# Retention in 64x64 tiles four at a time, and the layout of heads that goes with it

## The chip, the cores and the metric

The kernel runs on one core of a Trainium2 chip. A core has TensorE (PE, whose weight loads the profile lists apart as PEld), VectorE (DVE), ScalarE (ACT), GpSimd (POOL) and SyncE (SP), which issues the transfers between device memory and the on-chip memory SBUF. Matrix products land in PSUM, eight banks of 512 fp32 values in each of 128 partitions. The metric is the device time of one execution in microseconds; the time before is 725.04 us, the median of 4 runs (723.75 to 725.8).

## What is computed

Two blocks follow one another. First retention, with 4 batches, 8 heads, 768 positions and head size 64; then a gated feed-forward block over 3072 tokens of width 512 with 1536 hidden features.

```python
for t in range(S):
    state = gamma * state + einsum('bhd,bhe->bhde', k[:, :, t], v[:, :, t])
    y[:, :, t] = scale * einsum('bhd,bhde->bhe', q[:, :, t], state)
x = y.transpose(0, 2, 1, 3).reshape(B * S, H * D)
g = x @ w_gate
out = (g * sigmoid(g) * (x @ w_val)) @ w_out
```

q, k and v are fp32. The weights are float64 and reach the kernel as pairs of 32-bit words.

## The kernel before

**Retention by chunks.** The 768 positions of a batch are six chunks of 128. For a chunk, `scores` (L379) computes k times q per head into two banks (L385) and VectorE multiplies them by a table of decays (L391). `mix` (L431) computes y: the old state times q (L442, for all chunks but a batch's first), then the chunk's own v times scores (L446), which accumulates onto it; ScalarE copies y to the tile `xT` (L449), the input of the second block. `state` (L414) updates the running state (L424, L427, L429). Heads come in pairs: head 2n + i is at partitions 64i to 64i + 63 of pair n. A matmul of L385 has 64 rows and 128 columns of weights, one of L442 64 and 64, one of L446 and L424 128 and 64. Each fp32 matmul leaves two records in the profile, with two weight loads.

**Segments and stages.** The 24 chunks form four segments of six, three positions each of two batches. The program starts with retention of segment 0. Then the first up stage, `up(f)` for 12 blocks of hidden features, computes the products with w_gate and w_val (L515) by a scheme that needs seven products of sums of blocks where plain multiplication needs eight. A `down` stage multiplies by w_out by the same scheme (L709, L718). Later up stages, `up2`, apply the scheme twice (L626). Retention of segment s + 1 runs within the down stage of segment s: after each product `down` calls `step()`, and at counts listed in `DUE` (L841) `step()` runs one piece of `retention` (L453): scores of chunk n + 1, then mix, decay and state of chunk n. `sums_x` (L487) forms the sums of blocks of x on VectorE; in segment 0 it reads y from PSUM.

**Weights.** A piece of w_gate and w_val (128 hidden features, 1 MB in float64) is loaded by `load_piece` (L192), on SP's queue. It is turned to fp32 in three parts: `convert_a` on ScalarE (absolute value L242, copies of the sign words to two banks L246, low words L249), `convert_b` on VectorE (L259, L261, L265), `convert_c` on GpSimd (L274). Then `sums_t` on VectorE (L289) forms the sums of weight blocks, and `keep_wt` (L149) stores them to device memory for the later stages. The pieces of w_out take the same way.

**Order.** It is written out by hand: the string at L835 for segment 0 (s, m, t, x for scores, mix, state, sums; a, b, c, B, S, C, T for the parts of the conversion; the number is the chunk or the piece) and the table `beside` (L320) for the first up stage, whose entries run between products. Every engine works through its own instructions in that order, so an instruction that waits holds up those behind it. SP issues loads in order too, and a load into a buffer waits for GpSimd to be done with the buffer's last piece.

**Banks.** `bank(tag)` (L99) hands out banks in turn: scores 4 and 5, state 6, y 7, and 2 and 3 for the products wb and z of the down stage (L726, L758). In segment 0, y of the six chunks is in banks 0, 1, 2, 3, 7 and 6 (L436).

Of the kernel before, what the change touches and what calls it, by code (L numbers as in the profile page):

```python
# [12 lines left out]
U32 = mybir.dt.uint32  # L13
# [28 lines left out]
def tile_retnet_swiglu(  # L42
# [56 lines left out]
    def bank(tag):  # L99

        own = {"x": (0, 1), "wz": (2, 3), "s": (4, 5), "st": (6,), "y": (7,)}[tag]
        turn[tag] = turn.get(tag, -1) + 1
        return banks[own[turn[tag] % len(own)]]
# [88 lines left out]
    def load_piece(piece):  # L192

        kind, a, h = piece
        if kind == "up":
            new_wt(a)
            gate, val = (w[:, ts(a, P)].rearrange("(c p) f -> p c f", p=P)
                         for w in (w_gate, w_val))
            parts = [(val[:, ds(KH, KH)], 0), (val[:, ds(0, KH)], 1), (gate, 2)]
        else:  # L200
            top, low = (w_out[ts(a + FH * i, P)] for i in range(2))
            parts = ([(low[:, DH:], 0), (top[:, DH:], 1)],
                     [(top[:, :DH], 0), (low[:, :DH], 1)])[h]
        to, slot, n = span(piece)
        to = to[:, ds(slot, n)]
        if w_gate.dtype != F32:
# [4 lines left out]
        for src, i in parts:  # L211
            if w_gate.dtype != F32:
                src = src.bitcast(U32)
            if len(src.shape) == 3:
                c = src.shape[1]
                t = to[:, i:].rearrange("p a b -> p (a b)")[:, : c * src.shape[2]]
                t = t.rearrange("p (c f) -> p c f", c=c)
            else:
                t = to[:, i]
            nc.sync.dma_start(out=t, in_=src)  # L220
# [15 lines left out]

    def convert_a(piece, own, part=None):

        if piece in raw:
            d, lo, hi = words_of(piece)  # L240
            if part in (0, None):
                nc.scalar.activation(d, hi.bitcast(F32), AF.Abs)  # L242
            if part in (1, None):
                signs[piece] = []
                for i, o in enumerate(own):
                    nc.scalar.copy(banks[o], hi[:, ts(i, 512)].bitcast(F32))  # L246
                    signs[piece].append(banks[o])
            if part in (2, None):
                nc.scalar.activation(lo.bitcast(F32), lo, AF.Copy, scale=2.0 ** -51,  # L249
                                     bias=2.0)  # L250
# [18 lines left out]
    def convert_c(piece, halves=1):  # L269
        if piece in raw:  # L270
            d, lo, hi = words_of(piece)
# [107 lines left out]
    def scores(c):  # L379
        kt, qt = (pairs(t) for t in chunks[c][:2])  # L380
        sp = [bank("s") for i in range(2)]
        for n in range(NP):
            for i in range(2):
                r = ds(D * i, D)
                nc.tensor.matmul(sp[i][:, ts(n, P)], kt[r, n], qt[r, n],  # L385
                                 start=True, stop=True, skip_group_check=True)
# [27 lines left out]
    def state(c):  # L414
# [5 lines left out]
        st = bank("st")[:, : NP * D].rearrange("p (n e) -> p n e", n=NP)  # L420
# [552 lines left out]
```

## Time and profile before

| what | value |
|---|---|
| median of 4 runs | 725.04 us (723.75 to 725.8) |
| the profiled execution's own time | 724.39 us |
| its span | 722.6 us |
| TensorE: busy, share, instruction records | 708.0 us, 98%, 4544 |
| VectorE | 466.9 us, 65% |
| ScalarE | 240.0 us, 33% |
| GpSimd | 239.4 us, 33% |
| moved by DMA | 139.06 MB, mean 192 GB/s |

The span runs from the first to the last instruction of the program. The page says how long each engine was busy, and the chain of waits says what work, followed back from the end, set the time. A line such as L385 names the line of the kernel that issued an instruction. In a row of the timeline the bracket tells how long the engine was idle before, and what it then waited for. The granted clock of TensorE is full throughout.

In time order: segment 0's retention to 30 us, the first up stage to 149 us, the down stages (with retention) at 149 to 223, 319 to 395, 491 to 568 and 664 to 719 us, and the later up stages between them.

### The profile page before, as it was taken

The numbers are of one execution on the slowest core, as the hardware profiler recorded it, in microseconds if no ns is written. First come the engines' busy times: TensorE is split into PE (matmuls) and PEld (weight loads), VectorE is DVE, ScalarE is ACT, GpSimd is POOL, SyncE is SP. The second block draws the span as 40 slices with busy tenths as digits, with TensorE's granted clock in tenths as the row PEclk, the third lists the DMA queues.
The fourth block names the chain that finished last, engine by engine and source line by source line (L and its number), as shares of the span: only waits on it lengthen the run. The fifth ranks groups of instructions, "written<-read, shape, count | busy, mean of one in ns | idle before, by whom it ended". The sixth has DMA issues, their size and how long they took to land.

```text
span 722.6 us, 11724 instructions
## 1 busy us (share of the span) xinstructions
PE 708.0 (98%) x4544; PEld 616.5 (85%) x4544; DVE 466.9 (65%) x836; ACT 240.0 (33%) x484; POOL 239.4 (33%) x147
## 2 busy tenths in 40 slices
PE   7898999999999999999999999999999999999997
PEld 7654555578889999998888999998888999999886
DVE  3887998686858887875354575656652656667420
ACT  2668777411212232421121333331121233243000
POOL 0334444513101727470220445372210072735000
PEclk9999999999999999999999999999999999999999
DMA  9797897805997967742722555550473155630010
GB/s 320 241 376 266 281 295 223 312 14 189 393 351 278 332 208 268 240 168 88 257 94 102 182 202 206 198 182 16 139 255 132 59 200 200 203 134 1 9 51 30
DMA packets 60825, 139.06 MB, mean 192 GB/s; under 512 B 4577, under 2 KB 27617, under 8 KB 60769
## 3 DMA queue, kind: packets, MB, share of 16 engines
q1 hardware_dynamic: 57312, 132.01, 53.2%
q10 hardware_dynamic: 3456, 6.29, 2.3%
q8 instruction: 36, 0.59, 0.3%
q14 instruction: 21, 0.16, 0.1%
HBM read 101.72 MB, written 36.57 MB: 191 GB/s over the span
## 4 chain that ended last, share of the span: by engine, by line
PE 93%; DVE 1%; ACT 1%; issue 0%; DVEq 0%
PE bank L626 40%; PE bank L709 26%; PE bank L515 14%; PE bank L718 4%; PE bank L385 3%; PE bank L446 3%; PE bank L442 2%; PE bank L424 1%; DVE ring L289 0%; DVE iop L591 0%; ACT bank L246 0%; DVE hT L665 0%; ACT loadp L249 0%; DVE ring L265 0%; DVE ring L261 0%
## 5 line engine op out<-in xcount | busy, mean ns | idle before, releaser
L626 PE MATMUL bank<-loadp,ring 128*128 128x192 f32 x720 | 140.3, 327 | 0.0
L709 PE MATMUL bank<-wot,hsp 128*128 128x256 f32 x576 | 129.8, 382 | 0.0
L709 PEld LDWEIGHTS bank<-wot,hsp 128*128 128x128 f32 x576 | 108.0, 190 | 15.8 <-issue 0.5
L626 PEld LDWEIGHTS bank<-loadp,ring 128*128 128x128 f32 x720 | 120.6, 190 | 1.0 <-ACT midp L591 0.7
L591 DVE TENSOR_TENSOR iop<-bank,iop 128x384 f32<-128x384 f32 x144 | 79.6, 555 | 56.4 <-PE bank L626 53.0
L626 PE MATMUL bank<-xs,ring 128*128 128x192 f32 x432 | 87.9, 326 | 0.0
L661 POOL TENSOR_TENSOR hT<-iop 128x768 f32<-128x768 f32 x36 | 67.1, 1863 | 34.8 <-DVE iop L591 34.8
L591 ACT COPY hsp<-bank 128x384 f32<-128x384 f32 x90 | 43.0, 479 | 100.3 <-PE bank L626 89.5
L626 PEld LDWEIGHTS bank<-xs,ring 128*128 128x128 f32 x432 | 73.2, 190 | 0.0
L591 POOL TENSOR_TENSOR iop<-hsp,midp 128x768 f32<-128x768 f32 x9 | 16.3, 1814 | 165.7 <-ACT hsp L591 137.2
L626 PE MATMUL bank<-xT,ring 128*128 128x192 f32 x324 | 66.2, 327 | 0.8 <-DVE iop L591 0.8
L515 PE MATMUL bank<-xs,ring 128*128 128x384 f32 x192 | 64.7, 488 | 2.2 <-DVE xs L498 1.7
L709 PE MATMUL bank<-wot,hT 128*128 128x256 f32 x288 | 65.5, 381 | 0.0
L515 PEld LDWEIGHTS bank<-xs,ring 128*128 128x128 f32 x192 | 36.1, 190 | 28.9 <-issue 2.3
L709 PEld LDWEIGHTS bank<-wot,hT 128*128 128x128 f32 x288 | 54.3, 190 | 7.6 <-issue 0.2
L626 PE MATMUL bank<-hsp,ring 128*128 128x192 f32 x288 | 56.7, 326 | 0.5 <-ACT hsp L591 0.5
L626 PEld LDWEIGHTS bank<-xT,ring 128*128 128x128 f32 x324 | 54.8, 190 | 2.0 <-DVE iop L591 1.8
L515 PE MATMUL bank<-xT,ring 128*128 128x384 f32 x144 | 49.4, 488 | 1.5 <-DVE hT L552 1.5
L626 PEld LDWEIGHTS bank<-hsp,ring 128*128 128x128 f32 x288 | 48.4, 190 | 0.8 <-ACT hsp L591 0.8
L591 DVE TENSOR_TENSOR midp<-bank,midp 128x384 f32<-128x384 f32 x72 | 39.8, 554 | 13.8 <-PE bank L626 12.4
L768 DVE TENSOR_TENSOR iop<-bank,iop 128x256 f32<-128x256 f32 x12 | 5.1, 424 | 65.2 <-PE bank L709 48.2
L449 ACT COPY xT<-bank 128x512 f32<-128x512 f32 x24 | 14.1, 586 | 97.6 <-PE bank L446 97.6
(146 smaller groups left out, 987.0 us busy)
## 6 DMA issues: line engine op xcount, KB each, us to landing
ring<-unitt SPq DMA_DIRECT2D x50, 896.0 KB, 4.7
unitt<-ring SPq DMA_DIRECT2D x21, 896.0 KB, 6.0
unitb<-ring SPq DMA_DIRECT2D x12, 896.0 KB, 7.3
ring<-unitb SPq DMA_DIRECT2D x21, 512.0 KB, 6.0
out_dram<-iop ACTq DMA_DIRECT2D x24, 256.0 KB, 2.4
loadp<-in_w_val_dram SPq DMA_DIRECT2D x18, 256.0 KB, 3.7
loadp<-in_w_gate_dram SPq DMA_DIRECT2D x9, 512.0 KB, 6.5
midp<-in_w_out_dram SPq DMA_DIRECT2D x12, 256.0 KB, 6.6
```

The lines of the kernel that those rows point to most:

```text
L385: nc.tensor.matmul(sp[i][:, ts(n, P)], kt[r, n], qt[r, n], start=True, stop=True, skip_group_check=True)
L424: nc.tensor.matmul(st[ds(D * i, D), n], kd[:, h], vn[:, h], start=(n == 0), stop=True, skip_group_check=True)
L442: nc.tensor.matmul(y[r, ts(n, P)], prev[r, n], qd[r, n], start=(n == 0), stop=False, skip_group_check=True)
L446: nc.tensor.matmul(y[ds(D * i, D), ts(n, P)], vn[:, ts(2 * n + i, D)], a[i][:, n], start=(ci == 0 and n == 0), stop=True, skip_group_check ...
L449: nc.scalar.copy(xT[:, :, c // NCK % 2, ts(ci % L, P)], pairs(y))
L515: nc.tensor.matmul(o, w[:, slot, k], a[:, k], start=(start and k == 0), stop=(stop and k == KH - 1), skip_group_check=True)
L591: events.append((t, len(events), lambda: fn(*args, **kw)))
L626: nc.tensor.matmul(o[:, h], w[:, h, slot], rhs, start=(start and h == 0), stop=True, skip_group_check=True)
L661: by_block(9.5, 13.5, lambda r: pool(to[:, r], u2[:, r], p5[:, r], op=add))
L709: nc.tensor.matmul(o, a[:, k], wot[k][:, slot], start=(start and k == 0), stop=(k == FH - 1), skip_group_check=True)
L718: nc.tensor.matmul(o, a_dn(0, 0, u)[:, k], wot[k][:, B11], start=(k == 0), stop=(k == FH - 1), skip_group_check=True)
L768: tt(ev[0][:, DH:], wb, u2, op=ALU.add)
```

## The change

`scores` and the old state's part of `mix` issue matmuls of 64 rows and 64 columns of weights, so that four of them, two halves of the rows by two halves of the columns, follow one another. Scores are 16 instructions per chunk instead of 8; the others keep their number. y is in two banks, one for each i, of 256 columns each. In it, head 2n + i with n = 2h + b stands at partitions 64h, block b of bank i. `xT` takes this order, with one copy per bank. So the rows of w_gate and w_val are loaded in the same order: four transfers of 64 partitions for a piece instead of three of 128. `convert_a` works by halves of 512 columns that put the blocks of a half in their place, and writes the low words' result into the place of the high words. Banks are handed out anew: y has 6 and 7, state 6 for the first four chunks and 3 after that, wb and z of the down stage both 2; in segment 0 two chunks share a pair of banks.

```diff
@@ -98,7 +98,8 @@
 
     def bank(tag):
 
-        own = {"x": (0, 1), "wz": (2, 3), "s": (4, 5), "st": (6,), "y": (7,)}[tag]
+
+        own = {"s": (4, 5), "y": (6, 7)}[tag]
         turn[tag] = turn.get(tag, -1) + 1
         return banks[own[turn[tag] % len(own)]]
 
@@ -194,30 +195,34 @@
         kind, a, h = piece
         if kind == "up":
             new_wt(a)
-            gate, val = (w[:, ts(a, P)].rearrange("(c p) f -> p c f", p=P)
-                         for w in (w_gate, w_val))
-            parts = [(val[:, ds(KH, KH)], 0), (val[:, ds(0, KH)], 1), (gate, 2)]
-        else:
-            top, low = (w_out[ts(a + FH * i, P)] for i in range(2))
-            parts = ([(low[:, DH:], 0), (top[:, DH:], 1)],
-                     [(top[:, :DH], 0), (low[:, :DH], 1)])[h]
         to, slot, n = span(piece)
         to = to[:, ds(slot, n)]
-        if w_gate.dtype != F32:
+        bits = w_gate.dtype != F32
+        if bits:
             t = raw_places[kind].pop(0)
             if kind == "down" or a:
                 raw_places[kind].append(t)
             to = raw[piece] = t.bitcast(U32).rearrange("p (a b) -> p a b", a=n)
-        for src, i in parts:
-            if w_gate.dtype != F32:
-                src = src.bitcast(U32)
-            if len(src.shape) == 3:
-                c = src.shape[1]
-                t = to[:, i:].rearrange("p a b -> p (a b)")[:, : c * src.shape[2]]
-                t = t.rearrange("p (c f) -> p c f", c=c)
-            else:
-                t = to[:, i]
-            nc.sync.dma_start(out=t, in_=src)
+        parts = []
+        if kind == "up":
+
+
+            for w, i in ((w_val, 0), (w_gate, 2)):
+                w = w[:, ts(a, P)].rearrange("(h b j d) f -> h d b j f", h=2, b=2, j=2)
+                for h in range(2):
+                    t = to[ds(D * h, D), ds(i, 2)].rearrange("p i (b f) -> p i b f", b=2)
+                    if bits:
+                        parts.append((t.rearrange("p i b f -> p (i b) f"),
+                                      w[h].rearrange("d b j f -> d (b j) f")))
+                    else:
+                        parts += [(t[:, 1 - j if i == 0 else j], w[h][:, :, j])
+                                  for j in range(2)]
+        else:
+            top, low = (w_out[ts(a + FH * i, P)] for i in range(2))
+            parts = ([(to[:, 0], low[:, DH:]), (to[:, 1], top[:, DH:])],
+                     [(to[:, 0], top[:, :DH]), (to[:, 1], low[:, :DH])])[h]
+        for t, src in parts:
+            nc.sync.dma_start(out=t, in_=src.bitcast(U32) if bits else src)
 
 
 
@@ -234,20 +239,45 @@
         r = raw[piece].rearrange("p a (n two) -> p (a n) two", two=2)
         return d, r[:, :, 0], r[:, :, 1]
 
+    def by_half(piece):
+
+        d, lo, hi = words_of(piece)
+        for i in range(d.shape[1] // 512):
+            to, *src = (a[:, ts(i, 512)] for a in (d, lo, hi))
+            if piece[0] == "up":
+                to = to.rearrange("p (j b f) -> p j b f", j=2, b=2)
+                src = [a.rearrange("p (b j f) -> p j b f", j=2, b=2) for a in src]
+                if i == 0:
+                    src = [backwards(a) for a in src]
+            yield to, *src
+
+    def backwards(a):
+        (part, rows), (step, n), *rest = a.ap
+        return bass.AP(a.tensor, a.offset + step * (n - 1), [[part, rows], [-step, n], *rest])
+
     def convert_a(piece, own, part=None):
 
         if piece in raw:
             d, lo, hi = words_of(piece)
             if part in (0, None):
-                nc.scalar.activation(d, hi.bitcast(F32), AF.Abs)
+                for to, _, src in by_half(piece):
+                    nc.scalar.activation(to, src.bitcast(F32), AF.Abs)
             if part in (1, None):
                 signs[piece] = []
-                for i, o in enumerate(own):
-                    nc.scalar.copy(banks[o], hi[:, ts(i, 512)].bitcast(F32))
+                for o, (to, _, src) in zip(own, by_half(piece)):
+                    t = banks[o]
+                    if piece[0] == "up":
+                        t = t.rearrange("p (j b f) -> p j b f", j=2, b=2)
+                    nc.scalar.copy(t, src.bitcast(F32))
                     signs[piece].append(banks[o])
             if part in (2, None):
-                nc.scalar.activation(lo.bitcast(F32), lo, AF.Copy, scale=2.0 ** -51,
-                                     bias=2.0)
+
+                for i, (_, src, _) in enumerate(by_half(piece)):
+                    t = hi[:, ts(i, 512)]
+                    if piece[0] == "up":
+                        t = t.rearrange("p (j b f) -> p j b f", j=2, b=2)
+                    nc.scalar.activation(t.bitcast(F32), src, AF.Copy, scale=2.0 ** -51,
+                                         bias=2.0)
 
     def convert_b(piece, part=None):
 
@@ -268,7 +298,7 @@
 
     def convert_c(piece, halves=1):
         if piece in raw:
-            d, lo, hi = words_of(piece)
+            d, _, lo = words_of(piece)
             n = d.shape[1] // halves
             for i in reversed(range(halves)):
                 nc.gpsimd.tensor_tensor(d[:, ts(i, n)].bitcast(I32),
@@ -380,10 +410,11 @@
         kt, qt = (pairs(t) for t in chunks[c][:2])
         sp = [bank("s") for i in range(2)]
         for n in range(NP):
-            for i in range(2):
-                r = ds(D * i, D)
-                nc.tensor.matmul(sp[i][:, ts(n, P)], kt[r, n], qt[r, n],
-                                 start=True, stop=True, skip_group_check=True)
+            for h in range(2):
+                for i in range(2):
+                    r, m = ds(D * i, D), ds(D * h, D)
+                    nc.tensor.matmul(sp[i][m, ts(n, P)], kt[r, n, m], qt[r, n],
+                                     start=(n == 0), stop=True, skip_group_check=True)
         a = []
         for i in range(2):
             j = turn["a"] = turn.get("a", -1) + 1
@@ -417,7 +448,8 @@
             return
         vn, kd = chunks[c][2:]
         new = state_of(c)
-        st = bank("st")[:, : NP * D].rearrange("p (n e) -> p n e", n=NP)
+        st = banks[6 if c in first_chunks[:4] else 3][:, : NP * D]
+        st = st.rearrange("p (n e) -> p n e", n=NP)
         for n in range(NP):
             for i in range(2):
                 h = ts(2 * n + i, D)
@@ -432,23 +464,35 @@
         ci = c % NCK
         qd, vn = pairs(chunks[c][1]), chunks[c][2]
         a = att.pop(c)
-
-        y = banks[(0, 1, 2, 3, 7, 6)[first_chunks.index(c)]] if c in first_chunks else bank("y")
+        if c in first_chunks:
+
+            k = first_chunks.index(c)
+            y = [banks[b][:, ds(256 * (k % 2), 256)]
+                 for b in ((0, 1), (2, 3), (6, 7))[k // 2]]
+        else:
+            y = [bank("y")[:, :256] for i in range(2)]
+
+
+        y = [t.rearrange("p (b t) -> p b t", b=2) for t in y]
         if ci:
             prev = state_of(c, 1)
-            for n in range(NP):
-                for i in range(2):
-                    r = ds(D * i, D)
-                    nc.tensor.matmul(y[r, ts(n, P)], prev[r, n], qd[r, n],
-                                     start=(n == 0), stop=False, skip_group_check=True)
-        for n in range(NP):
+            for b in range(2):
+                for h in range(2):
+                    for i in range(2):
+                        r, n = ds(D * i, D), 2 * h + b
+                        nc.tensor.matmul(y[i][ds(D * h, D), b], prev[r, n], qd[r, n],
+                                         start=(b == 0), stop=False, skip_group_check=True)
+        for b in range(2):
             for i in range(2):
-                nc.tensor.matmul(y[ds(D * i, D), ts(n, P)], vn[:, ts(2 * n + i, D)],
-                                 a[i][:, n], start=(ci == 0 and n == 0), stop=True,
-                                 skip_group_check=True)
-        nc.scalar.copy(xT[:, :, c // NCK % 2, ts(ci % L, P)], pairs(y))
+                for h in range(2):
+                    n = 2 * h + b
+                    nc.tensor.matmul(y[i][ds(D * h, D), b], vn[:, ts(2 * n + i, D)],
+                                     a[i][:, n], start=(ci == 0 and b == 0), stop=True,
+                                     skip_group_check=True)
+        for i in range(2):
+            nc.scalar.copy(xT[:, ds(KH * i, KH), c // NCK % 2, ts(ci % L, P)], y[i])
         if c in first_chunks:
-            att[c] = pairs(y)
+            att[c] = y
 
     def retention(s):
 
@@ -491,7 +535,7 @@
 
         def b(i, h):
             y = att.get(first_chunks[2 * j + i])
-            return a(i, h) if y is None else y[:, ds(KH * h, KH)]
+            return a(i, h) if y is None else y[h]
 
         s1, s2, s3, s4 = (t[:, :, ts(j, P)] for t in xs)
         tt = nc.vector.tensor_tensor
@@ -723,7 +767,7 @@
                 step()
 
         def second(u):
-            z = bank("wz")[:, :DH]
+            z = banks[2][:, :DH]
             product(z, B21, a_dn(0, 1, u))
             to = iop[:, ts(2 * (u % 2), DM)]
             tt(to[:, :DH], z, first_dn.pop(u), op=ALU.add)
@@ -755,7 +799,7 @@
         elif u == 2 and s:
             first(u)
         cur = dict(hs)
-        wb = bank("wz")[:, :DH]
+        wb = banks[2][:, :DH]
         product(wb, T1, cur[1])
         p5 = tmp(2)
         nc.scalar.copy(p5, wb)
```

## The prediction

> **What bounds the kernel now.** I read the page's rows of the 40 slices first, then the chain of waits, then the work by ten-microsecond stretches, then ScalarE's timeline where weights arrive.
>
> ```profile
> span 722.6 us, 11724 instructions
> PE 708.0 (98%) x4544; PEld 616.5 (85%) x4544; DVE 466.9 (65%) x836; ACT 240.0 (33%) x484; POOL 239.4 (33%) x147
> PEclk9999999999999999999999999999999999999999
> ```
>
> TensorE is busy for 98% of the span at the full granted clock. Busy is not yet bound, so the chain of waits follows, for two steps of retention in the first down stage:
>
> ```profile
> 165.87 1.09 PE bank L385 x16
> 166.96 1.02 PE bank L442 x16
> 167.98 1.02 PE bank L446 x16
> 169.00 0.46 PE bank L424 x16
> 169.47 5.38 PE bank L709 x24
> ```
>
> Every piece is TensorE's own: scores (L385), old state's part of y (L442), the chunk's own part (L446), state (L424), then the down product. Whatever is saved here moves the end. The start and the first products are different. By stretches (us, then PE, PEld, DVE, ACT, POOL busy, clock, DMA share, GB/s):
>
> ```profile
> 30.00:40.00 10.00, 8.28 (x25) 4.67 (x26) 6.85 (x14) 5.93 (x10) 3.46 (x2) 1.00 0.76 234
> 40.00:50.00 10.00, 10.00 (x31) 5.35 (x30) 9.76 (x15) 6.64 (x11) 2.73 (x1) 1.00 1.08 374
> 50.00:60.00 10.00, 9.75 (x31) 5.43 (x29) 7.82 (x15) 6.46 (x10) 2.41 (x1) 1.00 0.95 324
> 60.00:70.00 10.00, 8.22 (x24) 4.39 (x24) 8.13 (x17) 9.26 (x15) 3.81 (x2) 1.00 0.83 280
> 70.00:80.00 10.00, 10.00 (x32) 6.00 (x32) 9.86 (x19) 8.03 (x15) 4.99 (x4) 1.00 0.82 270
> ```
>
> DMA is full (share 1.08) from 36 to 56 us, and PE idles 1.7 us in 30 to 40 and 1.8 us in 60 to 70. Who waits for DMA there, on ScalarE:
>
> ```profile
> 22.64 1.17 ACT L242 ACTIVATE ring<-loadp 128x1024 f32<-128x1024 f32 x1 [2.33 <-DMA loadp<-in_w_gate_dram]
> 28.69 1.18 ACT L242 ACTIVATE ring<-loadp 128x1024 f32<-128x1024 f32 x1
> 38.01 1.16 ACT L242 ACTIVATE ring<-loadp 128x1024 f32<-128x1024 f32 x1 [1.50 <-DMA loadp<-in_w_gate_dram]
> 43.42 1.16 ACT L242 ACTIVATE ring<-hsp 128x1024 f32<-128x1024 f32 x1
> ```
>
> These are the conversions of weight pieces 0 to 3. Pieces 0 and 2 wait for their load, and by the landing times in the trace (22.53, 28.47, 37.90, 43.31 us) pieces 1 and 3 are used within 0.25 us of landing. Pieces 4 and 5 land at 49.87 and 56.13 and are used at 53.77 and 57.35; from piece 6 on, a load has 4.4 to 7.7 us to spare. So a later load of the first four pieces is a later ScalarE, and behind its conversion in the same queue stand the copies that release TensorE (L449, L536, L541).
>
> **The change, part by part.**
>
> *Scores and old state.* The start times of single records tell how tiles overlap. Each fp32 matmul leaves two records. In L442 two 64x64 tiles start 7 ns apart and the next two 109 ns later; L446 (128x64) gives 109 ns as well, L385 (64x128) 111.6. Entering another tile shape costs more: 160 ns from the first pair to the second with 64 weight columns, 214 with 128, and 206 from the last pair to the next group. This rebuilds the rows: L385 is 214 + 6 x 111.6 + 206 = 1.09 us, L442 160 + 6 x 109 + 206 = 1.02.
> After, scores are 16 instructions per chunk, and both groups go in sets of four tiles. Two row tiles at once are shown by L385, two column tiles at once by L446; four at once are shown by no row. Lower bound: the set takes 109 ns. Upper: two pairs, 218. I take 112, since the second tile costs 7 ns of start only. Scores are then no faster in their eight sets, but their shape is now that of L442, and the change of shape between them goes: 160 + 6 x 109 + 109 = 0.92. L442 halves: 3 x 109 + 206 = 0.53. Together 1.46 instead of 2.11: 0.65 less. Scores alone save 0.07 (160 + 6 x 109 + 206 = 1.02), L442 alone 0.44 (160 + 2 x 109 + 206 = 0.58).
> Segments 1 and 3 have one step with scores alone, five with both, one with L442 alone: 0.07 + 5 x 0.65 + 0.44 = 3.8 us each. Segment 2, whose first two chunks have no old state, saves 3 x 0.07 + 3 x 0.65 + 0.44 = 2.6. Sum 10.2; at 112 ns for its 208 sets 0.6 less, 9.6. In the first down stage DMA share is 0.9 to 1.0 from 180 to 220 us and the last unit sum (VectorE L170) starts at 217.63 on a load landed at 214.61, so some of its 3.8 us is given back: I take 9.0. The first segment's six chunks count nothing: they wait for loads (TensorE's waits of 1.3 and 1.0 us for q_t).
>
> *Heads of y in two banks.* 24 copies of 128x512 (586 ns) become 48 of 128x256 (370 ns, as L761): 0.15 us per chunk on ScalarE, idle at L449 for 97.6 us in all: nothing. In the first segment two chunks now share two banks, so the second's y waits for the first's copies. For chunk 1 that is some 0.7 us before a wait of 1.3 us for q_t; for chunk 5 about 1 us, but its copy stands behind piece 1's conversion on ScalarE (28.69 to 30.88). Uncovered it would be 1 us; I take nothing.
> The down stage's wb and z now share bank 2 instead of alternating. z must follow VectorE's read of wb (L768), and the next wb the read of z (L729). The tightest places: L768 ends at 677.92, z starts at 679.81; L729 ends at 683.03, the next product starts at 684.99; in segment 0, 152.68 against 153.95. The cover is the product in between (2.7 us); without it 0.4 us each. Nothing.
>
> *Conversion by halves.* Two ScalarE operations of 512 for one of 1024, twice per piece: 2 x 0.56 against 1.06 from start to start, 0.1 us per piece, felt only where ScalarE sets the pace (60.2 to 64.5 us): 0.3 in all. VectorE and GpSimd do the same work.
>
> *Weight rows in another order.* A piece of 1 MB was 2 transfers of 256 KB and 1 of 512 KB over 128 partitions; it is now 4 of 256 KB, each to 64 partitions. SP issues one more (0.47 us) per piece, with room: it waits 35.6 us for GpSimd. What matters is the rate. By the row: in the full queue one 256 KB transfer lands 0.67 to 0.75 us after the one before (374 GB/s in 40:50); at that rate a piece stays at 2.8 us and costs nothing. The Trainium skill, "SBUF — State Buffer", section "Door 1: The DMA port swizzle", speaks against it: partitions 0 to 63 reach only 8 of 16 ports, measured 196 GB/s, at most 218; the section "Can I just issue two DMAs to hit both halves?" adds that a transfer to each half side by side brought +6%. No transfer of this trace goes to 64 partitions. By the rule 256 KB takes 262144 / 218 = 1.20 us (1.34 at 196), a piece 4.8, 2.0 more (2.5). I take the rule at 218.
> Transfers of the full queue land in the order of their issue, so each piece moves the later ones by 2.0:
> - Piece 0 lands at 24.5, piece 1 at 32.4 (was 28.47). From there ScalarE needs 0.6 (second half of the first conversion), 1.1 (signs) and 0.7 (chunk 5's copies), VectorE 0.45 (L498): the first T1 product starts at 35.3 where it started at 33.18, 2.1 late.
> - Piece 2 is issued after piece 0's last conversion, so 1.9 late, and lands at 37.9 + 1.9 + 2.0 = 41.8; 40.1 is wanted, and ScalarE's gaps there (0.8, and 0.6 ahead of TensorE) take most. Piece 3 lands behind it and a unit store (2.7): 41.8 + 2.7 + 4.8 = 49.3, wanted at 43.4 + 2.1 = 45.5; 3.8 late, 0.8 of it taken by the gap: +3.0.
> - Piece 4 lands 6.6 + 2.0 after piece 3, at 57.9, wanted at 53.8 + 5.1 = 58.9: in time. Piece 5 lands 6.3 + 2.0 after it, at 66.2, wanted at 57.4 + 5.1 = 62.5: 3.7 late, less 1.7 us of ScalarE idle before L246 and the 0.8 of PE's own wait: +1.2. From piece 6 on within slack.
> Sum 6.3, and all products behind follow one another on TensorE, so nothing takes it back. Ends: 0 and 11 (196 GB/s, no slack).
>
> *Sum.* -9.0 + 0.3 + 6.3 = -2.4. The profiled execution took 724.39 (span 722.6 and 1.8 around it), 0.65 under the median 725.04. Against the median: 722.6.
>
> **The rivals.**
> - *The half-partition transfers keep the rate of the row.* For: the old rate of 374 GB/s is itself not the ports' full rate, and neighbours in the queue may fill the other half. 725.04 - 9.0 + 0.3 = 716.3.
> - *Slower: the weight loads cost more than the packing saves.* One mechanism, DMA from 14 to 60 us, piece by piece on ScalarE. It decides from 8.7 us of delay on (9.0 - 0.3), 2.4 more than taken: pieces 0 to 5 are 24 transfers, so 0.1 us on each, 1.3 us per 256 KB, does it; at 196 GB/s and no slack 725.04 - 8.7 + 11 = 727.3. Against: two of the four waits have slack.
> - *The change doesn't do what it says: four tiles go as two pairs.* Then 208 sets x 109 ns = 22.7 us are added to -10.2: +12.5, with loads 725.04 + 12.5 + 6.6 = 744, without 738. Against: L385 and L446 show each half of it; the point from which it turns slower is 112 + 2.4 / 0.208 = 124 ns per set with the loads' delay, 112 + 8.7 / 0.208 = 154 without.
>
> **How the numbers follow.** Likeliest (half rate, partly hidden) 0.45, own range 719 to 726; full rate 0.30, 714 to 718; loads cost more 0.15, 725 to 729; pairs 0.10. About 0.2% (1.45 us) is what a measurement of this kernel can tell from no change. Faster: 0.8 of the first and all of the second, 0.66; rounded down for the small margin, 0.64. Same: 0.1. Slower: 0.26. The range leaves out the pairs and the edges: 714.5 to 729.
>
> **What would show it.** Sets of four records 109 to 115 ns apart and 0.5 us rows for the old state's matmuls: packing right. A 256 KB weight load landing 1.2 us after the one before, piece 1's conversion near 32 us and piece 3's near 49, and the first down-stage scores later than 159.4 by about 6: loads right. Landings 0.7 us apart and scores at 159.4: the first rival. A wait on bank 2 in a down stage, or a later end of the first stage for chunk 5's banks, would prove me wrong elsewhere.

## The result, and the profile after

The changed kernel takes 722.89 us (median of 31 runs, 719.94 to 727.11). The kernel before took 724.35 us on the same chips (median of 50 runs, 723.14 to 726.65). The ratio is 0.9983, with a 95% interval of 0.9975 to 0.9991: faster by 1.2 us (0.6 to 1.8), which is less than 0.2%. The profiled execution took 723.73 us (span 721.9), 0.84 above its median. Behind the first scores of the down stage it took as long as a second profiled execution of this kernel (553.3 us in both), so what varies is the start.

The page's first part, in the changed kernel:

```profile
span 721.9 us, 12562 instructions
PE 698.6 (97%) x4928; PEld 607.9 (84%) x4928; DVE 465.3 (64%) x836; ACT 245.0 (34%) x532; POOL 239.7 (33%) x147
```

TensorE is busy for 9.4 us less (708.0 before), and the span is only 0.7 shorter. The rest of the saving has turned into waiting. The chain of waits says where. First two steps of retention in the first down stage (start, duration, work; scores are now L416, the old state's part L483, the chunk's own part L489, state L456, the down product L753):

```profile
168.62 1.03 PE bank L416 x32
169.66 5.38 PE bank L753 x24
175.04 1.03 PE bank L416 x32
176.07 0.44 PE bank L483 x16
176.51 1.02 PE bank L489 x16
177.53 0.46 PE bank L456 x16
178.00 5.38 PE bank L753 x24
```

Scores and old state's part together take 1.03 + 0.44 = 1.47 us, where they took 1.09 + 1.02 = 2.11. From the first scores of this stage to the end the kernel before needed 722.6 - 159.40 = 563.2 us, the changed one 721.9 - 168.62 = 553.3: 9.9 less. But these scores start 9.2 us later. The same chain at the start, where all of the delay comes in (L559 are the products of the first up stage):

```profile
38.20 2.83 PE bank L559 x8
41.03 0.61 SPq L225
...
43.05 8.70 DMA hsp<-in_w_gate_dram
...
51.83 0.67 ACT ring L264
52.50 0.38 ACT iop L585
...
52.92 12.19 PE bank L559 x32
...
74.02 77.73 PE bank L559 x240
```

The block of 240 products, which started at 64.62, starts at 74.02. Before it, the chain now runs for 8.7 us through a transfer of w_gate (weight piece 3), its conversion (L264) and the copy behind that in ScalarE's order (L585). In the kernel before, no transfer stood in the chain there. Its rows to compare with:

```profile
64.62 77.91 PE bank L515 x240
...
159.40 1.09 PE bank L385 x16
```

The work by stretches (us, then PE, PEld, DVE, ACT, POOL busy, granted clock, DMA share, GB/s):

```profile
30.00:40.00 10.00, 8.18 (x92) 5.76 (x86) 7.64 (x16) 6.18 (x16) 3.83 (x3) 0.89 0.53 130
40.00:50.00 10.00, 10.00 (x32) 5.53 (x30) 7.54 (x13) 6.16 (x12) 2.40 (x1) 1.00 1.11 270
50.00:60.00 10.00, 7.13 (x18) 4.13 (x18) 5.55 (x12) 3.67 (x8) 2.38 (x1) 0.83 1.09 260
60.00:70.00 10.00, 8.97 (x28) 4.94 (x26) 6.74 (x13) 7.38 (x14) 2.41 (x1) 1.00 1.11 322
```

From 40 to 50 us the 16 DMA engines are as full as before (share 1.11, before 1.08) and move 270 GB/s where they moved 374. From 50 to 60 PE is idle for 2.9 us, and its granted clock is 0.83 on average, where it was 1.00. Who waits for transfers, on ScalarE (conversions of weight pieces 0 to 3, by halves; the first halves of pieces 0 and 2 are left out; what stands in brackets is the idle time before):

```profile
25.56 0.66 ACT L264 ACTIVATE ring<-loadp 128x512 f32<-128x512 f32 x1 [1.56 <-DMA loadp<-in_w_gate_dram]
33.39 1.29 ACT L264 ACTIVATE ring<-loadp 128x512 f32<-128x512 f32 x2
43.40 0.68 ACT L264 ACTIVATE ring<-loadp 128x512 f32<-128x512 f32 x1 [1.28 <-DMA loadp<-in_w_gate_dram]
49.28 0.67 ACT L264 ACTIVATE ring<-hsp 128x512 f32<-128x512 f32 x1 [0.90 <-DMA hsp<-in_w_val_dram]
51.83 0.67 ACT L264 ACTIVATE ring<-hsp 128x512 f32<-128x512 f32 x1 [1.88 <-DMA hsp<-in_w_gate_dram]
```

Piece 3, which waited for nothing before, now holds ScalarE up twice. TensorE's timeline shows the two places where it pays: scores of chunk 5, and the products behind L585.

```profile
21.11 1.10 PE L416 MATMUL bank<-hT 64*64 64x128 f32 x32 [1.26 <-DMA hT<-in_q_t_dram]
...
28.88 1.98 PE L416 MATMUL bank<-hsp 64*64 64x128 f32 x32 [3.25 <-DMA hsp<-in_q_t_dram]
...
38.20 5.40 PE L559 MATMUL bank<-xs,ring 128*128 128x384 f32 x16 [1.47 <-DVE xs L542]
...
47.31 2.74 PE L559 MATMUL bank<-xs,ring 128*128 128x384 f32 x8
52.92 4.44 PE L559 MATMUL bank<-xs,ring 128*128 128x384 f32 x8 [2.87 <-ACT iop L585]
```

After each of these two pauses the matmuls run slower: chunk 5's scores take 1.98 us where chunk 4's took 1.10, and the eight products take 4.44, where the same eight take 3.06 and 3.08 in runs with warm matmuls ahead of them (below). The kernel before, at chunk 5's scores and at its first T1 product:

```profile
24.72 1.16 PE L385 MATMUL bank<-hsp 64*128 64x128 f32 x16 [0.98 <-DMA hsp<-in_q_t_dram]
...
33.18 5.40 PE L515 MATMUL bank<-xs,ring 128*128 128x384 f32 x16 [1.72 <-DVE xs L498]
```

The delay of 9.2 us is made up so. The first T1 product (T1 is the first product that reads sums of x, the tile `xs`) starts at 38.20, before at 33.18: 5.0. Of this, 4.2 is the later start of chunk 5's scores (28.88, before 24.72) and 0.8 is their slower run; from their end to T1 both kernels need 7.3 us. The products behind piece 3 start at 52.92, before at 44.99: 7.9, so 2.9 more (the pause of 2.87). The slow products add 1.4: what follows them starts at 57.20, before at 47.89. A wait ahead of 74.02 adds 0.2, and as much comes back before the first down-stage scores.

### The profile page after: what moved, and what is told of

Read it like the earlier page. It is cut to its first block, busy times and chain, and to the rows that moved or that the text cites. A ratio compares the mean times of both kernels' runs of the same rounds, so it can differ in the third digit from the quotient of the medians.

```text
span 721.9 us, 12562 instructions
## 1 busy us (share of the span) xinstructions
PE 698.6 (97%) x4928; PEld 607.9 (84%) x4928; DVE 465.3 (64%) x836; ACT 245.0 (34%) x532; POOL 239.7 (33%) x147
## 4 chain that ended last, share of the span: by engine, by line
PE 90%; DVE 1%; DMA 1%; ACT 1%; issue 1%; SPq 0%; DVEq 0%; ACTq 0%
PE bank L670 40%; PE bank L753 26%; PE bank L559 13%; PE bank L762 4%; PE bank L416 3%; PE bank L489 3%; DMA hsp<-in_w_gate_dram 1%; PE bank L456 1%; PE bank L483 1%; DVE ring L319 0%; SPq L225 0%; DVE iop L635 0%; ACT bank L271 0%; DVE hT L709 0%; ACT loadp L279 0%
## 5 line engine op out<-in xcount | busy, mean ns | idle before, releaser
L753 PE MATMUL bank<-wot,hsp 128*128 128x256 f32 x576 | 129.8, 382 | 0.0
L753 PEld LDWEIGHTS bank<-wot,hsp 128*128 128x128 f32 x576 | 108.0, 190 | 15.9 <-issue 1.0
L559 PE MATMUL bank<-xs,ring 128*128 128x384 f32 x192 | 66.1, 497 | 5.0 <-ACT iop L585 2.9
L753 PE MATMUL bank<-wot,hT 128*128 128x256 f32 x288 | 65.5, 381 | 0.0
L559 PEld LDWEIGHTS bank<-xs,ring 128*128 128x128 f32 x192 | 37.0, 194 | 32.3 <-ACT iop L585 3.7
L753 PEld LDWEIGHTS bank<-wot,hT 128*128 128x128 f32 x288 | 54.3, 190 | 7.6 <-DVE midp L422 0.2
L559 PE MATMUL bank<-xT,ring 128*128 128x384 f32 x144 | 49.2, 488 | 1.6 <-DVE hT L596 1.6
L493 ACT COPY xT<-bank 128x256 f32<-128x256 f32 x48 | 15.5, 376 | 85.8 <-PE bank L489 83.8
```

The costliest lines, as they stand in the source:

```text
L493: nc.scalar.copy(xT[:, ds(KH * i, KH), c // NCK % 2, ts(ci % L, P)], y[i])
L559: nc.tensor.matmul(o, w[:, slot, k], a[:, k], start=(start and k == 0), stop=(stop and k == KH - 1), skip_group_check=True)
L753: nc.tensor.matmul(o, a[:, k], wot[k][:, slot], start=(start and k == 0), stop=(k == FH - 1), skip_group_check=True)
```

## The experiments

Packing and loads are two halves of the change, and the first two runs take one each.

### Packing alone

The matmuls are those of the changed kernel; weights are loaded and converted as before, in transfers to all 128 partitions. To keep the weights' row order, heads are paired differently on the way in, so that y comes out in the order of w's rows. Against the changed kernel:

```diff
-            for w, i in ((w_val, 0), (w_gate, 2)):
-                w = w[:, ts(a, P)].rearrange("(h b j d) f -> h d b j f", h=2, b=2, j=2)
...
+            gate, val = (w[:, ts(a, P)].rearrange("(c p) f -> p c f", p=P)
+                         for w in (w_gate, w_val))
+            parts = [(val[:, ds(KH, KH)], 0), (val[:, ds(0, KH)], 1), (gate, 2)]
...
-                        r, n = ds(D * i, D), 2 * h + b
+                        r, n = ds(D * i, D), 2 * b + h
...
-        a = a.reshape(B, NP, 2, NCK, P, D).transpose(0, 3, 2, 5, 1, 4)
+        a = a.reshape(B, 2, NP, NCK, P, D).transpose(0, 3, 1, 5, 2, 4)
```

> The changed kernel with the weights loaded and converted as before, to 128 partitions. The order of heads that the tiles of four want is had in another way: q, k, the decay table and the columns of v are paired as head i*4 + n instead of 2n + i, so the rows of the weights stay in their natural order. My theory (the tiles of four save 9 to 10 us, the half-partition loads cost about 9): some 9.5 us below before, near 715. If the cost of the changed kernel lies in the second bank of y, the shared banks or the doubled number of score matmuls, and not in the loads: no faster than the changed kernel, 722 to 724.

Measured: 716.60 us against 724.79 on the same chip, ratio 0.987 (0.9848 to 0.9892). The rows of the first down stage are those of the changed kernel (chain of waits; scores L387, old state L454):

```profile
168.39 1.03 PE bank L387 x32
169.42 0.44 PE bank L454 x16
```

From the first scores (161.98) to the end are 715.6 - 161.98 = 553.6 us, 9.6 less than before. The scores themselves start 2.6 us later than before in this execution. The same kernel was run again, beside other runs:

> The first experiment's kernel again on the same chip as the one with the warm matmuls, since the difference asked for is 1 us: 716 to 717.

Measured: 715.56 against 724.35, ratio 0.9882 (0.9867 to 0.9897); first scores at 160.28, 0.9 later than before, and again 553.7 us from there. So packing alone brings 8.2 to 8.8 us in all, and the start gives back 1 or more. The second run shows a wait that is new:

```profile
29.27 0.84 PE L454 MATMUL bank<-hsp,state 64*64 64x128 f32 x16 [1.09 <-ACT xT L464]
...
33.62 5.40 PE L530 MATMUL bank<-xs,ring 128*128 128x384 f32 x16 [1.00 <-DVE xs L513]
```

Chunk 5's y waits 1.09 us until ScalarE has copied chunk 4's out of the banks that the two now share. The first T1 product starts at 33.62, 0.44 after that of the kernel before. But this wait doesn't set it: T1 then waits another 1.00 us, for VectorE, and chunk 5's scores had started 0.45 late (25.17, before 24.72). In the first run they started 0.7 late and ran 0.7 slower (1.86 us), and T1 was 1.4 late. Why q, which they wait for, lands 0.4 to 0.7 us later in these two executions stays open.

### Half-partition loads alone

The kernel before, in which a weight piece is loaded in four transfers of 256 KB to 64 partitions each. It leaves out the order of columns that would go with this, so two halves of w_val's rows stand in each other's place and the output is another one; no instruction moves by it.

```diff
-            parts = [(val[:, ds(KH, KH)], 0), (val[:, ds(0, KH)], 1), (gate, 2)]
+            parts = []
+            for w, i in ((w_val, 0), (w_gate, 2)):
+                w = w[:, ts(a, P)].rearrange("(c h d) f -> h d c f", h=2, c=4)
+                parts += [(w[h], i, h) for h in range(2)]
...
-                c = src.shape[1]
-                t = to[:, i:].rearrange("p a b -> p (a b)")[:, : c * src.shape[2]]
-                t = t.rearrange("p (c f) -> p c f", c=c)
+                t = to[ds(D * hh, D), ds(i, 2)].rearrange("p j (c f) -> p (j c) f", c=2)
```

> The kernel before with one edit: each weight piece is loaded in four transfers of 256 KB to 64 partitions, as in the changed kernel; retention and the conversion are as before. The two halves of w_val's rows come out in each other's place, which moves no instruction but makes the output another one. My theory: the loads alone cost 8 to 9.5 us, 732 to 734, the first product of the second weight block near 53 instead of 45 us. If the conversion by halves or the retention's banks delay the changed kernel: below 1 us.

Measured: 734.99 against 724.79, ratio 1.0126 (1.0098 to 1.0154): 10.2 us slower. The first down-stage scores start at 168.88, 9.5 late, and 563.2 us follow, as before: all of it lies ahead of the down stages. The chain of waits is now a chain of transfers:

```profile
20.30 9.81 DMA hsp<-in_q_t_dram
30.25 2.08 PE bank L384 x16
...
43.24 8.17 DMA hsp<-in_w_gate_dram
51.43 8.29 DMA loadp<-in_w_gate_dram
59.74 9.14 DMA loadp<-in_w_gate_dram
```

The first row is not even a weight: it is q of chunk 5, to 128 partitions, in the queue among the halves.

### The number of transfers alone

Four transfers instead of three is part of that edit. Alone, to all 128 partitions:

```diff
-            parts = [(val[:, ds(KH, KH)], 0), (val[:, ds(0, KH)], 1), (gate, 2)]
+            parts = [(val[:, ds(KH, KH)], 0), (val[:, ds(0, KH)], 1),
+                     (gate[:, ds(0, KH)], 2), (gate[:, ds(KH, KH)], 3)]
```

> The kernel before with w_gate's piece in two transfers of 256 KB instead of one of 512, all still to 128 partitions, so four transfers per piece as in the changed kernel. My theory (the partitions set the rate): within 1 us of before, landings 0.7 us apart. If the number of transfers, and the window of eight open ones, sets it: several us slower, up to the 9 of the changed kernel.

Measured: 724.15, ratio 0.9998 (0.9983 to 1.0012). The number of transfers costs nothing that can be measured; what costs is that they go to 64 partitions.

### Scores as before

The changed kernel with scores of 64 rows and 128 columns of weights:

```diff
-            for h in range(2):
-                for i in range(2):
-                    r, m = ds(D * i, D), ds(D * h, D)
-                    nc.tensor.matmul(sp[i][m, ts(n, P)], kt[r, n, m], qt[r, n],
-                                     start=(n == 0), stop=True, skip_group_check=True)
+            for i in range(2):
+                r = ds(D * i, D)
+                nc.tensor.matmul(sp[i][:, ts(n, P)], kt[r, n], qt[r, n],
+                                 start=True, stop=True, skip_group_check=True)
```

> The changed kernel with the scores as before, 8 matmuls of 64 rows and 128 columns per chunk; the old state's part stays in tiles of four. My theory (a third of the saving is the change of tile shape that falls away between scores and old state): scores 1.09 and old state 0.58 us instead of 1.03 and 0.44, 0.2 us in 13 steps and 0.06 in 5, so 3 us slower than the changed kernel, near 726. If only the tiles of four in the old state count: equal to the changed kernel, 723.

Measured: 725.92 against 724.79, ratio 1.0012 (0.9995 to 1.0028): 3.0 us more than the changed kernel by the medians, 2.1 by the two ratios. The chain of waits has

```profile
178.25 1.09 PE bank L415 x16
179.34 0.60 PE bank L482 x16
```

Scores cost 0.06 more, and the old state's part, whose matmuls are the same as in the changed kernel, 0.16 more: it now follows scores of another tile shape. From the first scores to the end are 728.2 - 171.78 = 556.4 us, 3.1 more than in the changed kernel. So the scores' new shape pays mostly by what it saves the next group.

### Warm matmuls ahead of the slow products

The changed kernel with 12 matmuls of zeros, into a bank that is free there, ahead of the eight products that took 4.44 us:

```diff
+        if f == 1:
+            for _ in range(12):
+                nc.tensor.matmul(banks[7][:, :P], warm[:, :P], warm[:, :P], start=True,
+                                 stop=True, skip_group_check=True)
```

> The changed kernel with 12 matmuls of zeros (some 2.7 us at full clock) on TensorE just ahead of the product that waited 2.87 us for piece 3's conversion, into a bank that is free. My theory (that pause also costs the clock: the eight products behind it took 4.44 us instead of 2.74): they are back at 2.7, and the whole 1.3 to 1.7 us shorter, near 721.5. If the late loads alone set the time there, the next wait takes it up: unchanged, 723.

Measured: 722.62, ratio 0.9975 (0.9963 to 0.9986). As this couldn't be told from the changed kernel's 722.89, both were run again side by side:

> The changed kernel once more, for a comparison on the same chip with the next run. 722 to 723.5, and the granted clock under 0.9 between 50 and 60 us.

> The changed kernel with 12 matmuls of zeros ahead of the 8 products that ran at a lower granted clock, against the changed kernel on the same chip. Theory (the clock after the pause costs some 1.5 us of the start's 9.2): 0.8 to 1.6 us shorter than the run of the changed kernel beside it. Rival (the 8 products' time is taken up again by the next wait for a converted piece): within 0.4 us of it.

Measured: 723.56 for the changed kernel (0.9982, 0.9969 to 0.9995) and 723.02 with the warm matmuls (0.9976, 0.9963 to 0.9988). TensorE's timeline of the last:

```profile
48.48 2.94 PE L592 MATMUL bank<-warm 128*128 128x128 f32 x24 [0.15 <-DVE ring L295]
51.86 3.06 PE L559 MATMUL bank<-xs,ring 128*128 128x384 f32 x8 [0.44 <-ACT iop L585]
```

The eight products take 3.06 us, where they took 4.44 and, in the second run of the changed kernel, 4.54. From the first T1 product to the block of 240 the two runs with warm matmuls need 34.7 and 35.1 us, the two without 35.8 and 36.1: some 1.0 less in the traces. The medians differ by 0.3 and 0.5, and the intervals overlap. That these products are slow by the pause, and at full speed without it, is shown; that it costs the kernel's time as much is not.

The other slow place was tried in the kernel with packing alone: 8 warm matmuls ahead of chunk 5's scores (`v8` in the order of segment 0).

> The packing alone with loads as before (the first experiment's kernel), and 8 matmuls of zeros ahead of chunk 5's scores in segment 0, where TensorE paused 1.8 us for q_t and lost its clock (0.83 from 20 to 30 us; the scores took 1.86 us instead of 1.10). My theory: the first T1 product starts 1 to 1.4 us earlier, 33.3 instead of 34.6, and the whole ends 1 to 1.5 us below the first experiment, near 715. If chunk 5 waits for the shared banks of y and ScalarE rather than for the clock: unchanged, 716.6.

Measured: 716.08, ratio 0.989 (0.9874 to 0.9907), against 716.60 and 715.56 without.

```profile
23.97 2.05 PE L815 MATMUL bank<-warm 128*128 128x128 f32 x16
25.95 1.10 PE L388 MATMUL bank<-hsp 64*64 64x128 f32 x32
```

The scores ran in 1.10 us, but the first T1 product started at 34.41, no earlier (34.60 and 33.62 without). The theory isn't confirmed, and this run can't refute it either: the warm matmuls ran until 25.95, though q had landed at 24.95. What the scores gained in speed over the first run, 0.8 us, they lost by a start 0.5 later, and T1 came 0.2 earlier.

### Two queues

The changed kernel with every second transfer of a weight piece on GpSimd's queue, so that the two halves of the partitions can be filled side by side:

```diff
-        for t, src in parts:
-            nc.sync.dma_start(out=t, in_=src.bitcast(U32) if bits else src)
+        for n, (t, src) in enumerate(parts):
+            queue = nc.gpsimd if kind == "up" and n % 2 else nc.sync
+            queue.dma_start(out=t, in_=src.bitcast(U32) if bits else src)
```

> The changed kernel with the transfers to partitions 64 to 127 issued from GpSimd's queue and those to 0 to 63 from SP's, so that both halves can be under way at once. My theory[...]: no faster than the changed kernel, 722 to 726, the issue on GpSimd itself adding a little. If the two halves fill each other's idle ports: a piece in 3 us instead of 4.5 and 4 us or more below the changed kernel, 719 or less.

Measured: 728.37, ratio 1.007 (1.0044 to 1.0096), slower than the changed kernel; first scores start at 172.50. The two halves of a piece now come at different times: those of piece 3 on GpSimd's queue landed at 48.19 and 49.61, those on SP's at 54.41 and 55.72, so the piece is whole 4.0 us later than in the changed kernel (51.75). At the start, q of chunks 4 and 5 lands 6.7 and 4.7 us later than there, so this run mixes two effects; it shows no gain from a second queue, and doesn't measure the ports by themselves.

### The small parts

The kernel before, with three small edits of the change and nothing else: wb and z both in bank 2, y copied in two parts, and the two in-place steps of the conversion by pieces of 512 columns.

```diff
...
-        nc.scalar.copy(xT[:, :, c // NCK % 2, ts(ci % L, P)], pairs(y))
+        for i in range(2):
+            nc.scalar.copy(xT[:, ds(KH * i, KH), c // NCK % 2, ts(ci % L, P)],
+                           pairs(y)[:, ds(KH * i, KH)])
...
-            z = bank("wz")[:, :DH]
+            z = banks[2][:, :DH]
...
```

> The kernel before, with the three small edits of the change alone: the two projections' outputs both in bank 2, the conversion's two in-place steps by pieces of 512 columns, and y copied out of its bank in two copies of 256. Theory (the prediction cost these at nothing, because ScalarE is busy a third of the time and no bank that the down products wait for is touched): 0 to 0.5 us longer, 724 to 725. Rival: more ScalarE instructions lengthen the conversions of the first segment and with them the start: over 1.5 us longer, 726 or more.

Measured: 724.75 against 724.41, ratio 1.0001 (0.999 to 1.0013). Together they cost nothing that can be measured.

### q of chunk 5 ahead of piece 0

The largest term that the prediction had missed is the first T1 product, 5.0 us late. In VectorE's order, the mask of chunk 5's scores (L422) stands ahead of its part of piece 0's conversion (L295), and those scores waited for q:

```profile
30.91 1.29 DVE L422 TENSOR_TENSOR iop<-bank,tab 128x512 f32<-128x512 f32 x2 [2.90 <-PE bank L416]
32.11 1.28 DVE L295 SCALAR_TENSOR_TENSOR ring<-bank,ring 128x512 uint32<-128x512 uint32 x2
```

So the changed kernel was run with k and q of chunk 5 issued ahead of piece 0:

```diff
+    load_chunk(cs[5], early[20:22])
     load_next("up")
     load_chunk(cs[4], early[18:19])
-    load_chunk(cs[5], early[20:23])
+    load_chunk(cs[5], early[22:23])
```

> The changed kernel with k and q of chunk 5 issued ahead of weight piece 0 instead of behind it; nothing else differs. Theory (the start's 5.0 us come by q of chunk 5: its scores at 28.88 us, which TensorE reached after a pause of 3.25 us and ran at a lower granted clock, stand ahead of VectorE's part of piece 0's conversion in VectorE's order): q lands near 22.5, chunk 5's scores start near 25 and take 1.1 us, piece 0 lands near 26.8, and the first T1 product starts near 36 where it started at 38.2, 1.5 to 2.5 us earlier; 720.5 to 721.5. Rival (the landing of weight piece 0 itself sets the end of its conversion): the first T1 product starts at 38.5 to 39.5, and the time is 723 to 724.

Measured: 721.51 us, ratio 0.9958 (0.9945 to 0.9972), 1.4 to 2.1 less than the two measurements of the changed kernel. TensorE's timeline, and then VectorE's:

```profile
22.44 1.10 PE L416 MATMUL bank<-hsp 64*64 64x128 f32 x32
...
36.38 5.32 PE L559 MATMUL bank<-xs,ring 128*128 128x384 f32 x16
```

```profile
29.73 1.28 DVE L295 SCALAR_TENSOR_TENSOR ring<-bank,ring 128x512 uint32<-128x512 uint32 x2
```

Piece 0 landed 0.6 us later (26.09), and still VectorE's part of its conversion started 2.4 earlier and the first T1 product 1.8 earlier. One such row alone would not show much: a run with the warm matmuls, which come behind T1, had its T1 at 36.48 with the loads in the old order. The traces together do show it:

| execution | chunk 5's scores start, take (us) | first T1 product | from the scores' end |
|---|---|---|---|
| before | 24.72, 1.16 | 33.18 | 7.30 |
| changed | 28.88, 1.98 | 38.20 | 7.34 |
| changed, again | 28.73, 1.98 | 38.04 | 7.33 |
| changed with warm matmuls, again | 27.81, 1.35 | 36.48 | 7.32 |
| packing alone | 25.41, 1.86 | 34.60 | 7.33 |
| packing alone, again | 25.17, 1.10 | 33.62 | 7.35 |
| q ahead of piece 0 | 22.44, 1.10 | 36.38 | 12.84 |

With q in its old place, T1 follows the end of chunk 5's scores at a fixed distance, wherever the weights land (7.29 to 7.35 us in 12 of 13 executions, 7.71 with the loads alone). So the rival, by which piece 0's landing set T1, is out for the changed kernel. With q moved, that distance opens: the chain of waits now runs through the transfer of w_gate for piece 0, so now the landing does set it, and only 1.8 us is got back.

## Why the prediction was right, and where its terms were off

The prediction was 722.6 us with a sum of -9.0 + 0.3 + 6.3 = -2.4. In the two profiled executions the terms are -9.9, 0 and +9.2, -0.7 in all; at the medians the gain is 1.5 and, with 553.3 us behind the first scores and 1.8 around the span, the start is 722.89 - 1.8 - 553.3 - 159.4 = 8.4 late. The likeliest case, half rate and partly hidden, is what happened; its two large terms were both too small, by 0.9 and by 2 to 3, and the errors cancelled in part. That 722.89 lies so near to 722.6 is luck in part: the gain told was 2.4 us, the gain measured is 1.2 to 1.5, and the kernel before measured 0.7 lower than the 725.04 that was reckoned from.

**Packing.** Sets of four start 109.3 ns apart with 7 ns from tile to tile: the lower bound of 109, where 112 was taken. Step by step: scores with old state 1.47 us (told 1.46), scores alone 1.03 (told 1.02), old state alone 0.60 (told 0.58). At 109 ns the prediction's own sum was 10.2. The 0.6 allowed for a later load in the first down stage was not needed: there TensorE's pieces follow one another, 168.62 to 228.43 us, without a wait. The rival of two pairs (12.5 us more) is out. That a change of tile shape has a price of its own had been read from single records; the run with scores as before shows it (0.60 against 0.44 us for the same 16 instructions), and with the 0.06 us that scores themselves gain, 0.22 of the 0.64 us saved per step hang on the scores' shape.

**Rate of half-partition transfers.** The prediction had to choose between the trace's row, 0.67 to 0.75 us for each 256 KB, and an estimate of 1.20 us from the 218 GB/s that the Trainium skill gives as the most ("SBUF — State Buffer", section "Door 1: The DMA port swizzle"). In pieces 0 to 5 the 18 gaps between landings within a piece are 0.56 to 2.21 us, mean 1.16, which is 226 GB/s (220 to 241 in five more executions with halves). The rule was the right choice, if slightly low, and a reader of the trace alone would have told 716.3. That number belongs to the kernel with packing alone (716.60 and 715.56), so the first rival's sum came out for a kernel that loads as before.

**First T1 product: the step that failed.** Told 2.1 late, measured 5.0. The prediction moved the weight pieces only, took T1's path through the landing of piece 1 and ScalarE, and counted segment 0's retention at nothing because "they wait for loads". The path was another: in both kernels T1 waits for VectorE's sums, these for GpSimd's part of piece 0's conversion, that for VectorE's part (from its start to T1 6.09 us before and after), and in VectorE's order this part stands behind the mask of chunk 5's scores, which wait for q. And retention's loads lie in the same queue, among the halves: q of chunk 5 landed at 28.75 where it had landed at 24.59. Of these 4.2 us, 1.4 were there when q of chunk 4 had landed, just ahead of piece 0; 1.6 came within piece 0 (told 2.0), and 1.2 in the three transfers behind it, all to 128 partitions. With the scores' slower run, 0.8, this is the whole 5.0. The last run moved q ahead and got 1.8 back, before piece 0's landing became the limit.

**Piece 3's wait.** Told +3.0, measured 2.9 (2.87 of PE's idle time ahead of L585's reader). Landing told 49.3, measured 51.75, later than told by about as much as the start was.

**The granted clock.** Not in the prediction at all: it is 0.83 from 50 to 60 us, where it was 1.00. After the pause eight products took 4.44 us instead of some 3.1, and after q's pause scores 1.98 instead of 1.10. A wait of 2.9 us was priced at 2.9; it cost 4.3 where it stood (what follows started 1.4 later still).

**Piece 5.** Told +1.2; the gaps of TensorE from 65 to 74 us are those of before (1.55 and 0.65, before 1.55 and 0.47), so 0.2.

**What was told as nothing.** Bank 2 for wb and z, and y in two copies: nothing, by the run of the small parts. Conversion by halves: told 0.3, not to be seen. The shared banks in segment 0 were told as covered, 1 us if not: in the changed kernel 0.35 us before other waits; in the kernel with packing alone 1.09 us, and covered there too: from the end of chunk 5's scores to T1 it took 7.35 us, before 7.30.

**The slower rival** needed 8.7 us of delay to turn the sign. The start reached 8.4 to 9.2, and packing had become 9.9; so it came close.

**What stays open.** The parts do not add up: loads alone cost 10.2 us, packing alone saves 8.2 to 8.8, so both should be 1.4 to 2.0 slower, and the change is 1.2 to 1.5 faster. Some 1 us of it may be what packing alone gives back in its start, which late loads can cover. For the rest, how far starts vary is a candidate: with half loads and q in its old place, q of chunk 5 landed between 27.68 and 30.34 us in six executions, and the first down-stage scores of loads alone and of the change, 168.88 and 168.62, are alike in the traces. No run has told more.

## What to carry to other kernels

When a transfer in a shared queue gets slower, move everything behind it in that queue, not only its own readers: here the largest missed term came by a load that the change did not touch. A saving in a stretch where TensorE's work alone is the chain was kept whole here (9.9 us), but the layout that it demands of the data had its own price, and both are best measured apart: packing with loads as before, heads paired differently on the way in, takes 715.56 to 716.60 us and beats both kernels. A pause of TensorE can cost more than its length: 1.4 us more here, behind one of 2.9. And before a late load is priced, follow back what the next product really waits for.

## What the runs showed of the hardware

**A pause of under 3 us can slow the matmuls behind it.** The eight products behind L585, in five executions of the changed kernel and its variants, took 4.44, 4.54, 5.49, 4.33 and 4.45 us after pauses of 2.87, 3.07, 2.98, 3.06 and 2.28 us, and 3.08 (loads alone) and 3.05 (packing alone) after pauses of 2.53 and 1.21. With packing alone, chunk 5's scores took 1.86 us instead of 1.10 after a pause of 1.76. So the length of the last pause alone doesn't decide. The Trainium skill, "TensorE: Matmul & The Clock Gate", part 1, gives an idle window of about 3.4 us before the clock halves, counted from no fixed point. These pauses are shorter than such a window, and no run here shows the window itself; the measurement decides.

**Transfers to 128 partitions land more slowly among halves.** k and q of chunks 4 and 5 go to 128 partitions in every kernel. Where the weights do too, they landed 0.64 to 0.72 us after the transfer ahead of them (23 of 24 in six executions, one 1.05); among halves 0.85 to 1.76 us (24 in six executions). Why, no run told.

**The start of one program varies.** The first down-stage scores started at 168.62 and 168.77 in two executions of the changed kernel, at 168.00 and 166.20 with the warm matmuls, and the changed kernel's times spread over 7.2 us, where those of the kernel before spread over 3.5.
